# Gated mix on one core: nine stores of x moved behind the first burst of W', the last burst moved to piece 27, the rounding of sums and of u moved

## The chip, the core and the metric

One core of a Trainium2 chip runs the whole program. The metric is the device time of one execution in microseconds (us); the engines are named as in the profile: PE (TensorE, matmul), PEld (its weight loads), DVE (VectorE), ACT (ScalarE), POOL (GpSimd), SP (SyncE, which here only issues transfers). SPq, ACTq and POOLq are the same engines' instructions that issue transfers.

## What is computed

```python
x = A_x                                              # 1 x 2048 x 640
g = sigmoid((x * gate_w).sum(-1, keepdims=True))
# A: the real part of a DFT along the hidden axis and then the sequence
a, b = einsum("bsd,ed->bse", x, dft_hid_re), einsum("bsd,ed->bse", x, dft_hid_im)
y = einsum("ts,bse->bte", dft_seq_re, a) - einsum("ts,bse->bte", dft_seq_im, b)
# B: 32 heads pick 2 of 256 experts by keys in two halves
q = einsum("nd,dhc->nhc", x, w_q);  q1, q2 = q[..., :128], q[..., 128:]
s1, s2 = einsum("nhd,ed->nhe", q1, k1), einsum("nhd,ed->nhe", q2, k2)
...                                                  # top 2 of each, top 2 of their sums, softmax -> gates, experts
act = gelu(einsum("nd,nhkd->nhk", x, u[experts]))
out = einsum("nhk,nhk,nhkd->nd", gates, act, v[experts])
result = g * y + (1 - g) * out
```

## The kernel before: how the work is staged

All large products are in fp32, each operand taken apart into a rounded part (h) and a rest (l); a product is three matmuls (`mm3`, lines 138 to 142: h by h, h by l, l by h). ACT makes h, and DVE or POOL subtracts to make l (`split`, lines 133 to 136; the profile shows all of these under L135 and L136).

**The pieces.** The sequence transform is cut into 128 pieces (w, c, s): w is the real or imaginary matrix, c one of four blocks of 512 columns, s one of 16 tiles of 128 rows of x. Piece n (`seq_piece`, line 225) is 15 matmuls of 128x512 (five banks of 128 hidden features, three matmuls each) with x tile s, `X[s]`, as weights. The first four pieces run their matmuls in another order (L240). A column block is done when its 16 pieces are; the banks are then copied by ACT to the staging tile ST (L248), and only then may the next block's matmuls overwrite them. Block c ends with pieces 15, 31, 47 and so on. A piece's W tile (`wf`, 256 KB) is loaded five pieces ahead by SP (L173) and taken apart three pieces ahead into a ring of four places (`WS`).

**Hooks.** `at(n, f)` registers a step, and all steps of piece n are written into the engines' queues right after piece n's matmuls, in the order of registration. Every engine runs its queue strictly in that order. So this table of numbers, and not a scheduler, sets the order of all work around the change. Transfers issued by SP and ACT take turns on eight semaphores: a transfer is issued only after the one that had its semaphore before has landed.

**Before piece 30** the hooks fit in, beside the pieces:

- x: tiles 4 to 15 are loaded by SP (`load_x`, L284, one piece ahead of the split), taken apart by ACT and DVE three pieces before use (`split_x`), and summed for the gate by DVE (`gate_sum`, L314).
- Stores of x: room runs out later, so x tiles 0 to 8 are stored to a scratch in DRAM (`put_x`, L493, 640 KB each) at pieces 6, 8, 10, ..., 22, tiles 9 and 10 at piece 26; `get_x` (L497) loads them back, tiles 0, 1, 2 at pieces 28, 28, 29.
- W' = w_q by keys: 32 loads of 640 KB (`load_wq`, L396, tile `wq` or `wqu`) feed four bursts of eight (`w_part`, L405, 64 small matmuls) after pieces 10, 16, 22 and 28. Two banks take turns, and DVE transposes each pair of parts out of its bank into `wp` (L411) before the bank is used again. A burst makes two groups G of W'. Some loads borrow the room of an x tile: the last three (29, 30, 31) take those of X6, X7, X8.
- `split_w` takes group G apart into WH, WL (the profile's WU). For groups 4 to 7 `make_t` draws four sums and differences from W' (tile `tt`, one buffer; six DVE operations, L433 to L438) and takes each apart (tiles `tw`, in the room of X0 to X5, and a part of WU).
- u: five tiles are loaded (`load_u`, L446, two buffers) at pieces 22 to 26 and taken apart (`split_u`, tile UU) at pieces 24 to 28.
- x transposed: loaded at piece 22 (`load_xT`, L461), split at 27 (tiles xh, xl), and four sums of it are made by DVE at piece 28 (`sum_xT`, L480 to L483).

After piece 31 the first score products run on PE (`score_step`), between pieces 31 and 32 six matmuls of WU by xh and xl. From there on 16 tiles of scores, top-k picks, experts and the hidden transform run beside the rest of the pieces.

Of the kernel before, what the change touches and what calls it, by code (L numbers as in the profile page):

```python
# [8 lines left out]
F32 = mybir.dt.float32  # L9
# [8 lines left out]
P = 128  # L18
# [14 lines left out]
NG = HH // 8  # L33
# [73 lines left out]
def gated_mix_kernel(ctx: ExitStack, tc: tile.TileContext, xT, xn, dreT, dimT, wsre, wsim, wq, kT, uT, vv, gw, out):  # L107
# [14 lines left out]
    def bank(n, shape=(P, TC), dt=F32):  # L122
        return psum.tile(list(shape), dt, name=f"b{n}", tag=f"b{n}")

    def ps_t(shape, dt=F32):
        return bank(7, shape, dt)
# [6 lines left out]
    def split(f, h, l, eng):  # L133

        nc.scalar.activation(h, f, AF.Copy)  # L135
        eng.tensor_sub(l, f, h.bitcast(F32))  # L136
# [55 lines left out]
    def at(n, f, *args):  # L192
        then.setdefault(n, []).append(lambda: f(*args))
# [57 lines left out]
    for q in range(2 * NC):  # L251
        n = NT * (q + 1)
# [10 lines left out]
    p1 = p1_stack.enter_context(tc.tile_pool(name="p1", bufs=1, reuse_waits="tile"))  # L263
# [72 lines left out]
    t = ps_t([P, TC])  # L336
    for n in range(WARM):
        c = slice(0, 2 * P) if n < WARM - 1 else slice(2 * P, TC)
# [43 lines left out]
    NWQ = 4 * NG  # L382
    BURST = 8
# [14 lines left out]
    def w_part(m):  # L398
        G, n, r = m // 4, m // 2 % 2, m % 2
        if r == 0:  # L400
            wps[G, n] = bank(5 + n)
        ps = wps[G, n]
        w = wqs.pop(m)
        for j in range(4):
            nc.tensor.matmul(ps[32 * j:32 * j + 32, :HALF], kp[:, 8 * G // H, r, :], w[:, j], start=(r == 0),  # L405
                             stop=(r == 1))
        if r == 1:
            if n == 0:
                wp[G] = p1.tile([P, KD, P], F32, name="wp", bufs=2)
            t = wp[G].rearrange("p k (j c) -> p j k c", c=32)[:, 2 * n:2 * n + 2]  # L410
            nc.vector.transpose(t, wps.pop((G, n))[:, :HALF].rearrange("p (j k c) -> p j k c", j=2, c=32))  # L411
# [3 lines left out]
        k = slice(0 if G < NG // 2 else 2, KD)  # L415
        split(wp[G][:, k], WH[:, k, c], WL[:, k, c], nc.vector)

    TW, LEFT = {}, []

    def make_t(G):  # L420


        if not TW:
            f = [big.tile([P, 2 * D], F32R, name="tw", tag=f"X{n}") for n in range(6)]
            TW.update((n, [t[:, :PAIR].rearrange("p (k c) -> p k c", k=2) for t in f[2 * n - 2:2 * n]])
                      for n in (1, 2, 3))
            LEFT.extend(t[:, PAIR:] for t in f)
            TW[4] = WH[:, :2, TC:], WL[:, :2, TC:]
        c = slice(P * (G - NG // 2), P * (G - NG // 2 + 1))
        b12, b22 = (wp[G][:, k:k + 2] for k in (0, 2))  # L430
        (b11h, b21h), (b11l, b21l) = ([w[:, k:k + 2, c].bitcast(F32) for k in (0, 2)] for w in (WH, WL))
        t = p1.tile([P, 4, 2, P], F32, name="tt", tag="tt")
        nc.vector.tensor_sub(t[:, 0], b12, b11h)  # L433
        nc.vector.tensor_sub(t[:, 2], b22, b12)
        nc.vector.tensor_sub(t[:, 0], t[:, 0], b11l)
        nc.vector.tensor_sub(t[:, 1], b22, t[:, 0])
        nc.vector.tensor_sub(t[:, 3], b21h, t[:, 1])
        nc.vector.tensor_add(t[:, 3], t[:, 3], b21l)  # L438
        for n in range(1, 5):
            split(t[:, n - 1], *(w[:, :, c] for w in TW[n]), nc.vector)  # L440

# [54 lines left out]
        X[s] = place(tag)  # L496
        nc.sync.dma_start(X[s].bitcast(F32), xd[s])  # L497

    for s in range(9):
        at(6 + 2 * s, put_x, s)  # L500
    for s, tag in ((11, "xh"), (12, "xl")):
        at(s + 12, move_x, s, tag)
    for n in range(NT - 4):
# [5 lines left out]


    n = N0 - 1
    for B in range(NWQ // BURST):
        b = 10 + 6 * B
        for m in range(BURST * B, BURST * (B + 1)):
            at(b, w_part, m)
        for a in range(2):
            G = 2 * B + a
            at(b + (a if b < n - 1 else 0), split_w, G)
            if G >= NG // 2:
                at(min(b + 1, n - 1) + a, make_t, G)  # L520
    for b, m in enumerate((0, 1, 2, 3, 4, 5, 6, 7, 8)):
        at(b, load_wq, m)
    for m, b in enumerate((10, 10, 11, 11, 12, 12, 13, 14, 16, 16, 16, 17, 18, 19, 20, 20, 22, 22, 22, 22, 23, 24, 25), 9):
        at(b, load_wq, m)
    for s in range(9, AWAY):
        at(n - 3, put_x, s)
    for s, b in enumerate((28, 28, 29)):
        at(b, get_x, s, 6 + s)
    at(n - 7, load_xT, 0)
    for k in range(KD):  # L530
        at(n - 7 + k, load_u, k)
        at(n - 5 + k, split_u, k)
    for a in range(2):
        at(n - 2, split_xT, 0, a)
    at(n - 1, sum_xT, 0)
# [268 lines left out]
    for p in range(NP):  # L804
        n = N0 + 4 * p + min((p + 1) // 2, 3)
# [3 lines left out]
    for n in range(2 * NT + 3, 4 * NT + 3):  # L809
        s = n % NT  # L810
# [269 lines left out]
    for k, (n, m) in enumerate(((-1, 2), (0, 4), (5, 7), (7, 9), (10, 12))):  # L1080
        n, m = NT * (NC + 2) + n, NT * (NC + 2) + m
# [253 lines left out]
```

## Time and profile before

| | us |
|---|---|
| median of 3 runs | 756.03 |
| lowest and highest of them | 753.8 and 756.59 |
| the profiled execution's own time | 754.75 |
| its span (first to last instruction) | 753.0 |
| PE busy | 743.4 |
| DVE busy | 577.6 |
| ACT busy, POOL busy | 366.1, 341.7 |

A row of the timeline has start and duration in us, engine, line, operation, the tiles as out<-in, the shape and a count, and in brackets how long the engine stood idle before it and what ended that. Matmuls overlap, so a matmul's duration is longer than the distance to the next one. A row of the chain of waits has start, duration and what the time went to.

### The profile page before, as it was taken

Reading aid. Unit: us, or ns where it says so; the run is one execution under the profiler, and the core shown is the slowest. Engines: PE = TensorE matmul, PEld = TensorE weight load, DVE = VectorE, ACT = ScalarE, POOL = GpSimd, SP = SyncE. Lnnn points to the kernel's source line nnn. Section 1 sums busy time; section 2 is a strip of 40 time slices with the busy share of each in tenths; the row PEclk is TensorE's granted clock in tenths of the full one; section 3 lists DMA queues with packets and bytes.
Section 4 is the critical chain, followed back from the end, with each engine's and each line's share of the span. In section 5 each row is a group of like instructions: output and inputs, shape, how many; then the busy total and the mean of one; then the engine's idle time right before and its main releaser. Section 6 shows DMA issues by size and latency. Waiting matters only on the chain.

```text
span 753.0 us, 11145 instructions
## 1 busy us (share of the span) xinstructions
PE 743.4 (99%) x3923; PEld 604.8 (80%) x3923; DVE 577.6 (77%) x744; ACT 366.1 (49%) x664; POOL 341.7 (45%) x287
## 2 busy tenths in 40 slices
PE   9989999899999999999999999999999999999998
PEld 7857877688888888888888888888888888888887
DVE  7871364576899899999999888979899984357651
ACT  4334244542444755564553587533555653443451
POOL 5532433441523334244135555644456793487253
PEclk9999999999999999999999999999999999999999
DMA  9999979588575786863398766388856689775301
GB/s 340 407 399 340 380 303 342 163 245 251 146 205 129 177 262 162 220 173 124 102 353 308 188 157 191 111 265 293 297 184 196 222 268 352 210 243 171 111 29 71
DMA packets 84632, 171.11 MB, mean 227 GB/s; under 512 B 16096, under 2 KB 21600, under 8 KB 84320
## 3 DMA queue, kind: packets, MB, share of 16 engines
q1 hardware_dynamic: 70960, 146.13, 56.6%
q0 software_dynamic: 5472, 9.96, 8.4%
q10 hardware_dynamic: 8144, 14.31, 5.2%
q8 instruction: 31, 0.51, 0.3%
q14 instruction: 25, 0.20, 0.1%
HBM read 136.40 MB, written 32.39 MB: 224 GB/s over the span
## 4 chain that ended last, share of the span: by engine, by line
PE 91%; DMA 4%; DVE 3%; issue 1%; ACT 0%; SPq 0%; ACTq 0%
PE b L140 30%; PE b L142 29%; PE b L141 29%; PE b L405 2%; DMA xr<-in_xn 2%; DMA wq<-in_wq 1%; PE b L888 1%; DMA wf<-in_wsre 1%; DVE xr L314 1%; DVE X L136 0%; DVE WU L136 0%; ACT X L135 0%; DVE xf L481 0%; DVE wp L411 0%; DVE tw L136 0%
## 5 line engine op out<-in xcount | busy, mean ns | idle before, releaser
L140 PE MATMUL b<-WS,X 128*128 128x512 f32 x620 | 243.0, 392 | 2.5 <-ACT ST L248 2.5
L141 PE MATMUL b<-WS,X 128*128 128x512 f32 x620 | 241.3, 389 | 0.0
L142 PE MATMUL b<-WS,X 128*128 128x512 f32 x620 | 241.3, 389 | 0.0
L136 POOL TENSOR_TENSOR WS<-wf,WS 128x512 fp32r<-128x512 f32 x89 | 133.2, 1499 | 173.0 <-ACT WS L135 171.8
L140 PEld LDWEIGHTS b<-WS,X 128*128 128x128 f32 x620 | 116.4, 188 | 29.0 <-ACT ST L248 2.9
L142 PEld LDWEIGHTS b<-WS,X 128*128 128x128 f32 x620 | 116.4, 188 | 24.3
L141 PEld LDWEIGHTS b<-WS,X 128*128 128x128 f32 x620 | 116.4, 188 | 23.8
L135 ACT ACTIVATE WS<-wf 128x512 fp32r<-128x512 f32 x89 | 55.7, 626 | 84.1 <-PE b L142 55.6
L876 DVE TENSOR_TENSOR hot<-rows,wtab 128x1024 f16<-128x1024 f16 x64 | 57.9, 931 | 4.4 <-PE b L888 4.4
L136 POOL TENSOR_TENSOR xl<-xf,xh 128x640 fp32r<-128x640 f32 x16 | 26.8, 1675 | 73.5 <-ACT xh L135 67.1
L598 ACT ACTIVATE sc<-b 128x512 f32<-128x512 f32 x32 | 19.9, 621 | 78.8 <-PE b L142 75.0
L187 POOL DMA_DIRECT2D WS<-in_wsre x30 | 26.4, 880 | 60.6 <-ACT WS L185 59.3
L136 POOL TENSOR_TENSOR WS<-ra,WS 128x512 fp32r<-128x512 f32 x33 | 46.7, 1424 | 14.4 <-ACT WS L135 12.4
L846 ACT ACTIVATE b<-b,mask 128x128 f32<-128x128 f32 x128 | 43.1, 343 | 15.0 <-PE b L888 11.8
L135 ACT ACTIVATE WS<-ra 128x512 fp32r<-128x512 f32 x47 | 29.4, 631 | 42.4 <-PE b L142 28.2
L653 DVE TENSOR_TENSOR eq<-sc,mm 128x1024 f16<-128x1024 f32 x32 | 44.4, 1387 | 0.9
L660 DVE TENSOR_REDUCE tied<-eq 128x64 f32<-128x1024 f16 x32 | 39.0, 1218 | 0.9
L651 DVE TENSOR_REDUCE mm<-sc 128x64 f32<-128x1024 f32 x32 | 38.7, 1210 | 0.2
L213 DVE SCALAR_TENSOR_TENSOR ST<-ST,grow 128x512 f32<-128x512 f32 x40 | 30.4, 820 | 6.0 <-DMA grow<-gdr 4.7
L136 POOL TENSOR_TENSOR WP<-ra,WP 128x512 fp32r<-128x512 f32 x13 | 19.0, 1471 | 31.2 <-ACT WP L135 31.2
L876 DVE TENSOR_TENSOR hot<-hot,rows 128x1024 f16<-128x1024 f16 x32 | 31.5, 985 | 0.0
L140 PE MATMUL b<-WU,xh 128*128 128x512 f32 x80 | 31.2, 391 | 0.0
(218 smaller groups left out, 1442.9 us busy)
## 6 DMA issues: line engine op xcount, KB each, us to landing
X<-xd SPq DMA_DIRECT2D x36, 640.0 KB, 6.2
wq<-in_wq SPq DMA_DIRECT2D x28, 640.0 KB, 9.2
wf<-in_wsim SPq DMA_DIRECT2D x64, 256.0 KB, 4.7
wf<-in_wsre SPq DMA_DIRECT2D x63, 256.0 KB, 6.4
ra<-pd SPq DMA_DIRECT2D x40, 256.0 KB, 3.1
pd<-ST ACTq DMA_DIRECT2D x35, 256.0 KB, 3.9
WS<-in_wsre POOLq DMA_DIRECT2D x30, 256.0 KB, 6.0
xd<-X SPq DMA_DIRECT2D x11, 640.0 KB, 8.6
```

Source lines behind the costliest of these rows:

```text
L135: nc.scalar.activation(h, f, AF.Copy)
L136: eng.tensor_sub(l, f, h.bitcast(F32))
L140: nc.tensor.matmul(o, wh, ah, start=first, stop=False, skip_group_check=more)
L141: nc.tensor.matmul(o, wh, al, start=False, stop=False, skip_group_check=more)
L142: nc.tensor.matmul(o, wl, ah, start=False, stop=last, skip_group_check=more)
L187: nc.gpsimd.dma_start(l, (wsre, wsim)[w][c, s], accum_op=OP.add)
L213: nc.vector.scalar_tensor_tensor(f, f, -1.0 if w else 1.0, g, op0=OP.mult, op1=OP.mult)
L651: nc.vector.tensor_reduce(m, sc, op=OP.max, axis=AX.X)
L653: nc.vector.tensor_tensor(eq, sc, m[:, :, None].to_broadcast([P, HH, E]), op=OP.is_equal)
L660: nc.vector.tensor_reduce(tied[:, s, ib, :], eq, op=OP.add, axis=AX.X)
L846: nc.scalar.activation(f[:, :, n], f[:, :, n], AF.Copy, scale=mask4[:, n:n + 1])
L876: nc.vector.tensor_tensor(o, a, b, op=op)
```

## The change

The nine stores of x tiles 0 to 8 move from pieces 6, 8, ..., 22 to pieces 11, 12, 14, 15, 17, 18, 19, 20, 21. The last burst moves from after piece 28 to after piece 27. Both groups of a burst are taken apart at the burst's own piece. `make_t` is cut in two: the sums of group G are drawn at piece b or b + 1 and are taken apart one piece later (`split_t`). The u tiles are loaded at pieces 20 to 24 and taken apart at 22 to 26. Tile 0 of x is loaded back at piece 27 (1 and 2 stay at 28 and 29). No work is added or left out.

```diff
     def make_t(G):
...
-        t = p1.tile([P, 4, 2, P], F32, name="tt", tag="tt")
+        tts[G] = t = p1.tile([P, 4, 2, P], F32, name="tt", tag="tt")
...
+    def split_t(G):
+        c, t = slice(P * (G - NG // 2), P * (G - NG // 2 + 1)), tts.pop(G)
         for n in range(1, 5):
             split(t[:, n - 1], *(w[:, :, c] for w in TW[n]), nc.vector)
...
-    for s in range(9):
-        at(6 + 2 * s, put_x, s)
+    for s, b in enumerate((11, 12, 14, 15, 17, 18, 19, 20, 21)):
+        at(b, put_x, s)
...
-    for B in range(NWQ // BURST):
-        b = 10 + 6 * B
+    for B, b in enumerate((10, 16, 22, 27)):
         for m in range(BURST * B, BURST * (B + 1)):
             at(b, w_part, m)
-        for a in range(2):
-            G = 2 * B + a
-            at(b + (a if b < n - 1 else 0), split_w, G)
+        for G in (2 * B, 2 * B + 1):
+            at(b, split_w, G)
             if G >= NG // 2:
-                at(min(b + 1, n - 1) + a, make_t, G)
+                at(b + G % 2, make_t, G)
+                at(b + G % 2 + 1, split_t, G)
...
-    for s, b in enumerate((28, 28, 29)):
+    for s, b in enumerate((27, 28, 29)):
         at(b, get_x, s, 6 + s)
...
-        at(n - 7 + k, load_u, k)
-        at(n - 5 + k, split_u, k)
+        at(n - 9 + k, load_u, k)
+        at(n - 7 + k, split_u, k)
```

Lines behind `make_t` move by two or three in the numbering (L493 becomes L496, L446 becomes L449, L480 becomes L483). On PE alone one thing moves: the 15 matmuls of piece 28 stand behind the last burst and no longer ahead of it. POOL's queue stays as it is, and behind piece 32 every queue does.

The first place is SP's queue from piece 8 to the first burst at piece 10. Before (xd<-X is a store of an x tile, xr the load of one, here of tiles 12, 13 and 14; wqu and wq are loads for W', wf a W tile):

```order
L493 DMA xd<-X 128x1280
L284 DMA xr<-in_xn 128x640
L396 DMA wqu<-in_wq 128x1280
L173 DMA wf<-in_wsre 128x512
L284 DMA xr<-in_xn 128x640
L173 DMA wf<-in_wsre 128x512
L493 DMA xd<-X 128x1280
L284 DMA xr<-in_xn 128x640
L396 DMA wq<-in_wq 128x1280 x2
```

The same place now:

```order
L284 DMA xr<-in_xn 128x640
L396 DMA wqu<-in_wq 128x1280
L173 DMA wf<-in_wsre 128x512
L284 DMA xr<-in_xn 128x640
L173 DMA wf<-in_wsre 128x512
L284 DMA xr<-in_xn 128x640
L396 DMA wq<-in_wq 128x1280 x2
L173 DMA wf<-in_wsre 128x512
L496 DMA xd<-X 128x1280
```

The stores of pieces 8 and 10 (and the one of piece 6, further up) are gone from in front of the x loads; the first store now stands behind the two wq loads and the W tile that follow.

The second place is DVE's queue after the last burst. Before, from the rounding of group 6's sums (tw and WU<-tt) on; xf are the sums of x transposed:

```order
L136 TENSOR_TENSOR tw<-tt,tw 128x2x128 x3
L136 TENSOR_TENSOR WU<-tt,WU 128x2x128
L136 TENSOR_TENSOR WU<-wp,WU 128x3x128
L136 TENSOR_TENSOR UU<-uf,UU 128x256
L480 TENSOR_TENSOR xf<-xf 128x256
L481 TENSOR_TENSOR xf<-xf 128x256
L482 TENSOR_TENSOR xf<-xf 128x256
L483 TENSOR_TENSOR xf<-xf 128x256
L433 TENSOR_TENSOR tt<-wp,WU 128x256
L434 TENSOR_TENSOR tt<-wp 128x256
L435 TENSOR_TENSOR tt<-tt,WU 128x256
L436 TENSOR_TENSOR tt<-wp,tt 128x256
```

The same place now:

```order
L136 TENSOR_TENSOR WU<-wp,WU 128x3x128
L136 TENSOR_TENSOR tw<-tt,tw 128x2x128 x3
L136 TENSOR_TENSOR WU<-tt,WU 128x2x128
L433 TENSOR_TENSOR tt<-wp,WU 128x256
L434 TENSOR_TENSOR tt<-wp 128x256
L435 TENSOR_TENSOR tt<-tt,WU 128x256
L436 TENSOR_TENSOR tt<-wp,tt 128x256
L437 TENSOR_TENSOR tt<-WU,tt 128x256
L438 TENSOR_TENSOR tt<-tt,WU 128x256
L483 TENSOR_TENSOR xf<-xf 128x256
L484 TENSOR_TENSOR xf<-xf 128x256
L485 TENSOR_TENSOR xf<-xf 128x256
```

Group 7's sums (the second run of L433 to L438) now stand ahead of the sums of x transposed, and the rounding of u is no longer in between.

The third place is SP's queue around the third burst at piece 22, where the loads for the last burst and those of u stand. Before (xf is x transposed, uf a tile of u):

```order
L493 DMA xd<-X 128x1280
L396 DMA wq<-in_wq 128x1280 x4
L461 DMA xf<-in_xT 128x640 x2
L446 DMA uf<-in_uT 128x256
L173 DMA wf<-in_wsre 128x512
L396 DMA wq<-in_wq 128x1280
L446 DMA uf<-in_uT 128x256
```

Now:

```order
L496 DMA xd<-X 128x1280
L449 DMA uf<-in_uT 128x256
L173 DMA wf<-in_wsre 128x512
L396 DMA wq<-in_wq 128x1280 x4
L464 DMA xf<-in_xT 128x640 x2
L449 DMA uf<-in_uT 128x256
L173 DMA wf<-in_wsre 128x512
L396 DMA wq<-in_wq 128x1280
L449 DMA uf<-in_uT 128x256
```

Two u loads moved ahead of the four wq loads, so the u load behind x transposed is now the third, which waits for a buffer of the two.

More of the change, by code (lines that the diff above doesn't have):

```diff
@@ L416, in split_w @@
         split(wp[G][:, k], WH[:, k, c], WL[:, k, c], nc.vector)
-    TW, LEFT = {}, []
+    TW, LEFT, tts = {}, [], {}
     def make_t(G):
```

## The prediction, made before the changed kernel was run

> **What bounds the kernel now.** I read the page's first part, then who PE waited for, then the places of those waits in the timeline, and the chain of waits at each.
>
> ```profile
> span 753.0 us, 11145 instructions
> PE 743.4 (99%) x3923; PEld 604.8 (80%) x3923; DVE 577.6 (77%) x744; ACT 366.1 (49%) x664; POOL 341.7 (45%) x287
> ```
> ```profile
> PE b L405 <- DVE wp L411: 3.0, 1, 3.0
> PE b L140 <- ACT ST L248: 2.5, 1, 2.5
> PE b L339 <- PEq L1327: 0.8, 1, 0.8
> ```
>
> PE is the bound, and in all it stood still three times: 0.8 us at the start, once in a W' burst, and once before a matmul that wanted a bank. The change adds and removes no matmul, so what it can win is at most those two stalls. The timeline places them:
>
> ```profile
> 18.76 0.39 PE L140 MATMUL b<-WS,X 128*128 128x512 f32 x1
> ...
> 42.34 0.39 PE L142 MATMUL b<-WS,X 128*128 128x512 f32 x1
> 42.65 2.36 PE L405 MATMUL b<-wq,kp 128*32 128x320 f32 x32
> 48.05 1.82 PE L405 MATMUL b<-wq,kp 128*32 128x320 f32 x24 [3.03 <-DVE wp L411]
> ```
> ```profile
> 137.00 0.39 PE L142 MATMUL b<-WU,xl 128*128 128x512 f32 x1
> 139.85 0.50 PE L140 MATMUL b<-WS,X 128*128 128x512 f32 x1 [2.46 <-ACT ST L248]
> ```
>
> The first stands in the middle of the first burst (3.03 us), the second ahead of piece 32 (2.46 us). Between 18.76 and 42.34 lie seven pieces, 105 matmuls, so one every 23.58 / 104 = 0.227 us and 3.40 us a piece; I use this pace below. 3.03 + 2.46 = 5.49 us is 0.73% of the time. A measurement of this kernel can tell about 0.5% (3.8 us) from no change, so both stalls must go for a clear gain.
>
> The chain of waits at the first stall:
>
> ```profile
> 36.77 8.43 DMA xr<-in_xn
> ...
> 45.23 0.75 ACT X L135
> ...
> 45.99 0.83 DVE X L136
> 46.82 0.73 DVE xr L314
> ...
> 47.56 0.44 DVE wp L411
> ...
> 48.05 2.36 PE b L405 x32
> ```
>
> PE waits for a transpose that frees the bank. DVE's queue has x tile 13's subtraction and tile 12's gate sum ahead of that transpose, and tile 13 landed at 45.20. Nothing on PE or DVE is slow here: a load of x is late. The transfers in that stretch (20 to 60 us):
>
> ```profile
> DMA packets 5073, 16.19 MB, mean 405 GB/s; under 512 B 565, under 2 KB 565, under 8 KB 5069
> ...
> xd<-X SPq DMA_DIRECT2D x5, 640.0 KB, 9.1
> ```
>
> The chain at the second stall, from the last transpose of the last burst to the bank's copy:
>
> ```profile
> 121.16 4.49 PE b L405 x64
> 125.68 0.52 DVE wp L411
> ...
> 131.75 0.34 DVE UU L136
> 132.09 0.35 DVE xf L480
> ...
> 134.35 0.42 DVE xf L483
> 134.78 0.34 DVE tt L433
> ...
> 136.74 0.44 DVE tt L438
> ...
> 139.22 0.59 ACT ST L248
> ```
>
> DVE works without a gap from 125.68 to 137.18. ACT can round group 7's sums only when DVE has made them, and the copies of the banks (L248) stand behind that rounding in ACT's queue. PE wanted the bank right after 137.00.
>
> **Part 1: the stores behind the first burst.** The stores of pieces 6 and 8 leave the queue ahead of x tile 13 (that of piece 10 stood behind it already). Each is 640 KB, 655,360 bytes; at 405 GB/s that is 1.62 us, two 3.24 us. The queue is full over this stretch and lands in order, so I let tile 13 land 3.24 us earlier, at 41.96. ACT is free by then: its row for piece 13's W tile was held behind x tile 12, which comes earlier by the same two stores.
>
> ```profile
> 42.17 0.74 ACT L135 ACTIVATE X<-xr 128x640 fp32r<-128x640 f32 x1 [3.33 <-DMA xr<-in_xn]
> 42.82 0.61 ACT L135 ACTIVATE WS<-wf 128x512 fp32r<-128x512 f32 x1
> ```
>
> These move to 38.93 and 39.58; the ring place that the second wants is free once piece 9 has run, at 42.65 - 3.40 = 39.25. Then the chain above runs as it stands, 3.24 us earlier: the transpose ends at 48.00 - 3.24 = 44.76. PE asks for the bank at 42.65 + 2.36 = 45.01. So the stall goes, with 0.25 us to spare: **-3.03 us**, and the bound on the other side is what the margin is worth (below, the gate sum).
>
> **Part 2: the end of the stage.** Two things shift against each other. PE: before, pieces 29, 30, 31 and six matmuls lay between the burst and the demand, 51 x 0.227 = 11.6 us; now piece 28 lies there too, 66 x 0.227 = 15.0 us. DVE and ACT: from the last transpose's start to the end of the first bank's copy went 139.81 - 125.68 = 14.1 us. The rounding of u (0.34) and the four sums of x transposed (134.78 - 132.09 = 2.69) no longer stand ahead of group 7's sums; that leaves 14.1 - 3.0 = 11.1. The copy would be ready 3.9 us ahead of the demand: **-2.46 us**. What is late next is the copy's own source, the bank that PE itself finishes in piece 31, and that costs nothing as the copies follow PE bank by bank. The five stores that ACT issues at piece 28 now stand behind the last W' rounding; two of them wait for transfers that SP issues behind the burst. I take nothing for that: it has the 3.9 us as cover, and costs what goes beyond it.
>
> **Part 3: what moves into the middle.** The stores don't vanish. From piece 17 to 21 there are five, one a piece; a piece then carries 640 + 640 + 256 KB for stores, W' and W. That is 1,572,864 bytes, 3.88 us at 405 GB/s against 3.40 us of PE: the queue grows by 0.5 us a piece, 2.4 us in all. The third burst needs load 23, the first of these two:
>
> ```profile
> 81.00 1.97 SPq L396 DMA_DIRECT2D wq<-in_wq  x2
> ```
> ```profile
> DMA to landing us min/median/max: 10.8/11.2/11.6
> ```
> ```profile
> 96.10 4.44 PE b L405 x64
> ```
>
> It landed at 91.8; its matmuls are the last eighth of the burst, at 96.10 + 3.9 = 100.0. Of these 8.2 us the earlier PE takes 3.0 and the fuller queue 2.4; 2.8 are left. Cost 0, on the other side 1 us if my queue is off by half again. W tiles are loaded five pieces (17 us) ahead: 0.
>
> The last burst comes 3.40 us earlier against its loads, and 3.03 for the first stall. Its last load, 31:
>
> ```profile
> 111.95 0.43 SPq L396 DMA_DIRECT2D wq<-in_wq  x1
> ```
> ```profile
> DMA to landing us min/median/max: 5.8/5.8/5.8
> ```
>
> It landed at 117.8 and was wanted at 121.16 + 3.9 = 125.1. Now it is wanted at 125.1 - 3.4 - 3.0 = 118.7, so even if it doesn't move with the rest it is in time by 0.9 us; it should move, since it waits for piece 24 on PE, and u loads that are ahead of it run on DVE's work of the same earlier pieces. Cost 0. The u rounding moves to pieces 22 to 26, among stretches in which DVE waited:
>
> ```profile
> 113.39 0.43 DVE L136 TENSOR_TENSOR UU<-uf,UU 128x256 fp32r<-128x256 f32 x1 [2.32 <-ACT UU L135]
> ```
>
> Five at 0.43 us fit into waits like that one. Rounding both groups at the burst's own piece on DVE only swaps neighbours. Moving the reload of x tile 0 to piece 27 costs nothing: it stays behind the burst that frees its room, and is wanted at piece 32.
>
> **The sum.** 754.75 (the profiled execution's own time, 1.75 over its span) - 3.03 - 2.46 = 749.3 us. The profiled execution was a quick one: the median of the three runs is 1.28 over it, and the mean of all four 755.3. From that mean: 755.3 - 5.5 = **749.8 us**, my number.
>
> **Rivals.**
>
> *The gate sum holds the transpose.* The same operation takes two times on DVE:
>
> ```profile
> 43.69 1.90 DVE L314 CUSTOM_DVE_ANT_0 xr<-xr,gwb 128x640 f32<-128x640 f32 x1
> ...
> 46.74 0.82 DVE L314 CUSTOM_DVE_ANT_0 xr<-xr,gwb 128x640 f32<-128x640 f32 x1
> ```
> ```profile
> 43.51 1.40 POOL L136 TENSOR_TENSOR WS<-wf,WS 128x512 fp32r<-128x512 f32 x1 [2.40 <-ACT WS L135]
> 49.76 1.29 POOL L136 TENSOR_TENSOR WS<-wf,WS 128x512 fp32r<-128x512 f32 x1 [4.85 <-ACT WS L135]
> ```
>
> 1.90 us where a subtraction runs on POOL, 0.82 where POOL is idle, as it was for tile 12's sum. If the earlier x loads push that sum onto POOL's subtraction, the transpose comes 1.08 us later, and with 0.25 us to spare 0.8 us of the first stall stays: 750.6. Against it: ACT's rounding ahead of that subtraction moves up as well, by my times POOL is done at 39.58 + 0.69 + 1.40 = 41.7 and the sum starts at 46.74 - 3.24 = 43.5. [...] Chance 0.10.
>
> *One stall stays whole.* If x tile 13 is held by something else than the queue's length (a buffer, a semaphore), the first stall stays: 755.3 - 2.5 = 752.8. If ACT is held at its five stores for over 3.9 us, the second does: 752.3. For it: margins of 0.25 and 3.9 us are thin against landings of 8 us. Chance 0.11.
>
> *The gain is given back.* The fuller queue lets the third burst wait for load 23 by as much as was won: 755.3. This takes 8 us more lateness than I find. Chance 0.06.
>
> *Slower: the last burst waits for load 31.* SP issues in order, and each of the last three loads stands behind a u load that waits for DVE to have done with an older u tile:
>
> ```profile
> SPq L446 <- DVE UU L136: 3.6, 3, 1.9
> ```
>
> That was 3.6 us in all. DVE now has the sums of groups 4 and 5 around these roundings. If each of the three waits grew to 4 us (a group's sums take 2.4, 134.78 to 137.18, and their rounding comes on top), load 31 would be issued 8.4 us later than now, less the 3.0 of the earlier PE: it lands at 123.2 against 118.7, and 4.5 us of the 5.5 are lost. It turns slower once load 31 lands later than 118.7 + 5.5 = 124.2; with waits of 6 us it lands at 129.2, 10.5 late: 760.3. Against it: in the old order DVE was through with groups 4 and 5 by 113.39 and idle ahead of a u tile (the row above). Chance 0.05.
>
> That the change doesn't do what it says is ruled out by the order: no store stands ahead of tile 13 any longer.
>
> **How the numbers follow.** Both stalls go: 0.68, about 749.8, with 1 us of unknown cost above and the scatter of the runs (753.8 to 756.59) about it. Of that, some 0.08 would show as less than 0.5%. Gate sum: 0.10, nearly all still faster. One stall stays: 0.11, within 0.5%. Given back: 0.06, within. Slower: 0.05. So faster 0.69, same 0.26, slower 0.05. The range goes from 753.8 - 5.5 - 0.5 = 747.8 up to 753.0, over the case of one stall; it leaves out the last two cases.
>
> **What would show it.** Right: PE waits only for its start, the first burst takes 4.4 us as the others do, x tile 13 lands near 42, and the matmul behind the score products has no wait. Wrong: a row of PE waiting for L411 at the first burst (the gate sum at 1.90 beside it or the x load late), for L248 ahead of piece 32, or for `wq` at 93 to 97 or 114 to 119 us. A stall of over 1 us anywhere on PE behind 140 us would mean that work beside the pieces lived on the old delays.

## The result and the profile after

750.11 us median of 6 executions (749.8 to 750.29), before 755.95 us median of 6 (753.8 to 756.98): the ratio is 0.9927, 95% interval 0.9912 to 0.9942. The profiled execution took 750.29 us with a span of 748.5; that of before took 754.75 with 753.0. The two traces thus differ by 4.46 us, the two medians by 5.84. Both numbers need an explanation.

The page of after, its first lines, and who PE waited for (us in total, times, the longest):

```profile
span 748.5 us, 11144 instructions
...
PE 743.3 (99%) x3923; PEld 604.3 (81%) x3923; DVE 579.4 (77%) x744; ACT 365.3 (49%) x664; POOL 342.6 (46%) x287
```
```profile
PE b L140 <- ACT ST L248: 1.1, 2, 0.7
PE b L339 <- PEq L1329: 0.8, 1, 0.8
```

PE's busy time is what it was (743.4 before), so the 4.5 us came out of PE's waits. The wait for L411 is gone. The wait for a bank copy (L248) is still there, twice now, 1.1 us in all.

**The first stall is gone, by the predicted chain.** PE at the first burst, and ACT and DVE ahead of it:

```profile
42.42 3.98 PE L405 MATMUL b<-wq,kp 128*32 128x320 f32 x56
46.22 0.72 PE L405 MATMUL b<-wqu,kp 128*32 128x320 f32 x8
46.87 0.50 PE L140 MATMUL b<-WS,X 128*128 128x512 f32 x1
```
```profile
41.56 0.74 ACT L135 ACTIVATE X<-xr 128x640 fp32r<-128x640 f32 x1 [1.75 <-DMA xr<-in_xn]
```
```profile
42.34 0.83 DVE L136 TENSOR_TENSOR X<-xr,X 128x640 fp32r<-128x640 f32 x1 [0.42 <-ACT X L135]
43.08 0.82 DVE L314 CUSTOM_DVE_ANT_0 xr<-xr,gwb 128x640 f32<-128x640 f32 x1
...
43.82 0.51 DVE L411 STREAM_TRANSPOSE wp<-b 128x320 f32<-128x320 f32 x1
```

ACT starts on x tile 13 at 41.56, where before it started at 45.23: the tile landed 3.67 us earlier (predicted 3.24). The gate sum ahead of the transpose took 0.82 us, not the 1.90 of the rival, and the transpose was there at 43.82 for a bank that PE wanted near 42.42 + 2.36 = 44.78 (2.36 is what a burst's first 32 matmuls took before).

**A wait that was not there before.** PE at piece 16:

```profile
64.81 0.50 PE L140 MATMUL b<-WS,X 128*128 128x512 f32 x1 [0.65 <-ACT ST L248]
```

The chain of waits behind it, and ACT at the same place before:

```profile
44.62 8.97 DMA xd<-X
...
53.68 9.85 DMA wf<-in_wsre
...
63.64 0.63 ACT WS L135
64.27 0.49 ACT ST L248
```
```profile
64.32 0.63 ACT L135 ACTIVATE WS<-wf 128x512 fp32r<-128x512 f32 x1 [1.24 <-PE b L142]
64.95 2.64 ACT L248 ACTIVATE ST<-b 128x512 f32<-128x512 f32 x4
```

The first of the moved stores took 8.97 us to land. The load of a W tile was issued behind its landing, took 9.85 us itself, and its rounding stands ahead of the bank copies in ACT's queue. Before, the same rounding ran at 64.32 and was itself waiting for PE, which was 3 us later then. That W tile (the 18th load of its kind in both traces) was issued at 52.64 before and landed 10.3 us later, at 62.9, which left it 1.4 us; now it landed at 63.5, and PE was some 3 us earlier. So the moved stores made a W tile 0.6 us late where the earlier PE had used up the slack.

**The second stall shrank from 2.46 to 0.48 us.** PE ahead of piece 32, then ACT (ACTq rows are the issuing of DMAs), DVE and POOL behind the last burst:

```profile
134.52 0.39 PE L142 MATMUL b<-WU,xl 128*128 128x512 f32 x1
135.39 0.50 PE L140 MATMUL b<-WS,X 128*128 128x512 f32 x1 [0.48 <-ACT ST L248]
```
```profile
122.21 0.74 ACT L135 ACTIVATE xh<-xf 128x640 fp32r<-128x640 f32 x1 [1.34 <-DMA xd<-X]
122.37 0.83 ACTq L223 DMA_DIRECT2D pd<-ST  x2
...
123.23 0.61 ACTq L223 DMA_DIRECT2D pd<-ST  x1
...
123.88 2.68 ACTq L223 DMA_DIRECT2D pd<-ST  x2
126.61 1.04 ACT L135 ACTIVATE tw<-tt 128x256 fp32r<-128x256 f32 x3 [2.50 <-issue]
```
```profile
123.05 0.55 DVE L136 TENSOR_TENSOR WU<-wp,WU 128x384 fp32r<-128x384 f32 x1
127.06 1.69 DVE L136 TENSOR_TENSOR tw<-tt,tw 128x256 fp32r<-128x256 f32 x3 [3.46 <-ACT tw L135]
128.67 1.50 DVE L136 TENSOR_TENSOR WU<-tt,WU 128x256 fp32r<-128x256 f32 x1
```
```profile
123.03 3.52 POOL L136 TENSOR_TENSOR xl<-xf,xh 128x640 fp32r<-128x640 f32 x2 [5.79 <-ACT xh L135]
126.51 1.29 POOL L136 TENSOR_TENSOR WS<-wf,WS 128x512 fp32r<-128x512 f32 x1
128.55 1.34 POOL L136 TENSOR_TENSOR WS<-wf,WS 128x512 fp32r<-128x512 f32 x1 [0.76 <-ACT WS L135]
```

DVE, which had no gap here before, stands 3.46 us: group 6's rounding on ACT comes late, behind five stores whose issuing takes 4.1 us (0.83 + 0.61 + 2.68) and behind a rounding of x transposed that waited for a landing. When DVE goes on, its operations run beside POOL's subtractions and take 1.69 and 1.50 us. Before, the same rows took 1.09 and 0.42:

```profile
129.86 1.09 DVE L136 TENSOR_TENSOR tw<-tt,tw 128x256 fp32r<-128x256 f32 x3
130.86 0.42 DVE L136 TENSOR_TENSOR WU<-tt,WU 128x256 fp32r<-128x256 f32 x1
```

From the start of the last transpose (119.79) to the end of the first copy (135.34) that makes 15.55 us instead of the predicted 11.1. The demand came 15.0 us after the burst, as predicted, so half a microsecond of the stall was left.

In the traces: -3.03 - 2.46 + 0.65 + 0.48 = -4.36 us, of 4.46 measured.

**A margin thinner than I thought.** The last burst and its last loads in the trace of after:

```profile
L405 PE MATMUL b<-wq,kp x64: 432/432/457, 115.2 to 119.3; 128*32 128x320 f32 x64
L396 SPq DMA_DIRECT2D wq<-in_wq x2: 382/402/423, 109.6 to 111.3; - x2
...
DMA to landing us min/median/max: 4.5/5.8/7.1
```

Load 31 was issued at 111.3 and landed at 118.4; the last eighth of the matmuls began at 115.2 + 56/63 x 4.1 = 118.8. PE did not wait, but with 0.4 us to spare, not 0.9. The load did not move with PE as I had thought it should: it was issued 0.7 us earlier than before and took 7.1 us to land instead of 5.8. The rival "slower" was nearer than I had priced it.

### The profile page after: what moved, and what is told of

Its sections match the earlier page's. It is cut to its first block, busy times and chain, and to the rows that moved or that the text cites. A ratio compares the mean times of both kernels' runs of the same rounds, so it can differ in the third digit from the quotient of the medians.

```text
span 748.5 us, 11144 instructions
## 1 busy us (share of the span) xinstructions
PE 743.3 (99%) x3923; PEld 604.3 (81%) x3923; DVE 579.4 (77%) x744; ACT 365.3 (49%) x664; POOL 342.6 (46%) x287
## 4 chain that ended last, share of the span: by engine, by line
PE 92%; DMA 5%; DVE 2%; SPq 0%; ACT 0%; issue 0%; ACTq 0%; DVEq 0%
PE b L140 29%; PE b L142 29%; PE b L141 29%; DMA xd<-X 2%; PE b L240 2%; DMA wf<-in_wsre 2%; PE b L405 1%; PE b L890 1%; DMA pd<-ST 1%; DVE WU L136 0%; PE b L339 0%; DVE tt L436 0%; DVE tw L136 0%; SPq L173 0%; DVE UU L136 0%
## 5 line engine op out<-in xcount | busy, mean ns | idle before, releaser
L142 PE MATMUL b<-WU,xl 128*128 128x512 f32 x80 | 31.1, 389 | 0.0
```

The source lines that it names most:

```text
L142: nc.tensor.matmul(o, wl, ah, start=False, stop=last, skip_group_check=more)
```

## The experiments

The theory after the result: the stores alone remove the first stall, the earlier burst with the new rounding order alone removes the second, and what is left over comes from the moved stores (piece 16) and from ACT's own five stores (piece 32). The rivals: the gain lies elsewhere than in these stalls, or the second stall is set by the late transfers and by POOL, not by who issues ACT's stores. The last question, opened by the first experiments, was why medians move by more than the stalls do.

**e0: the kernel before, a second profile.** No edit.

> The kernel before, profiled a second time, to see where its scatter of 3.2 us (753.8 to 756.98) lies. Theory: in the two stalls, so that first plus second stall differ from 5.5 us by as much as this execution's time differs from 754.75. Rival: the stalls are 3.0 and 2.5 again and the difference lies elsewhere.

756.03 us. PE's stalls are 2.3 and 2.7 us, 0.5 us less than in the first trace, and yet this execution took 1.28 us longer. Behind the first stall its second row of the burst (24 matmuls) took 3.43 us, against 1.82 us for the same 24 in the first trace of before. The windows show why (the columns are the window, its length, the busy time of PE, PEld, DVE, ACT and POOL with their instructions, the granted clock, the DMA share and GB/s):

```profile
47.42 3.43 PE L405 MATMUL b<-wq,kp 128*32 128x320 f32 x24 [2.27 <-DVE wp L411]
```
```profile
44.00:48.00 4.00, 1.73 (x28) 0.53 (x23) 3.35 (x7) 0.94 (x2) 0.27 (x1) 0.92 1.03 396
48.00:52.00 4.00, 4.00 (x35) 1.70 (x28) 1.02 (x3) 1.78 (x3) 1.27 (x1) 0.65 1.02 403
```

The granted clock falls behind the stall. Work lost, in full-clock time: 0.08 x 4.00 + 0.35 x 4.00 = 1.72 us. In the first trace both windows stand at 1.00. So the time of before is not its stalls alone: some executions pay a clock drop on top. The theory as stated failed here, and the drop was added to it.

**e1: the stores alone.** Against before:

```diff
-    for s in range(9):
-        at(6 + 2 * s, put_x, s)
+    for s, b in enumerate((11, 12, 14, 15, 17, 18, 19, 20, 21)):
+        at(b, put_x, s)
```

> Only the nine stores moved, the rest as before. Theory: the first stall goes (3.0 to 0), the new wait before piece 16 is there (about 0.6), the second stall stays (2.5): 3.0 - 0.6 = 2.4 us faster in the profiled execution, about 752.4. Rival (the first stall went because both groups of a burst are now rounded at once): the first stall stays at 3.0 and there is no gain.

753.55 us (12 executions, 753.14 to 754.25), ratio 0.9963 (0.9949 to 0.9978). In its profile the first stall is gone, PE waits 0.45 us ahead of piece 16 and 2.62 ahead of piece 32. So the new wait at piece 16 belongs to the stores, and the second stall to the other part. Behind the second stall the clock drops here:

```profile
136.00:140.00 4.00, 3.01 (x8) 2.41 (x9) 3.04 (x5) 4.00 (x11) 2.52 (x3) 0.66 0.39 56
```

**e2: all but the stores.** Against after:

```diff
-    for s, b in enumerate((11, 12, 14, 15, 17, 18, 19, 20, 21)):
-        at(b, put_x, s)
+    for s in range(9):
+        at(6 + 2 * s, put_x, s)
```

> Everything changed but the stores, which stay at pieces 6, 8, ..., 22. Theory: the first stall stays at 3.0, there is no wait before piece 16, and the second stall is 0.5 or less: 2.0 to 2.5 us faster in the profiled execution, about 752.5. Rival: the second stall went only because PE came to it earlier or the transfers were differently placed, so it stays over 1.5 us here and the gain is under 1 us.

754.11 us (12 executions, 752.34 to 756.1), ratio 0.9972 (0.9954 to 0.999). First stall 3.6 us, with a clock drop behind it; second 0.6; none ahead of piece 16. Alone, the two parts bring 2.26 and 1.70 us in the medians, together 5.84: more than their sum, since each alone leaves a stall of 2.6 us or more, behind which the clock can still drop. Both profiled executions took longer than expected (753.2 us for 752.4, 755.3 for 752.5): their stalls came within 0.6 us of what was expected, but the theory had no clock drops.

**e3: one store of the two.** Against before:

```diff
-        at(6 + 2 * s, put_x, s)
+        at(11 if s == 1 else 6 + 2 * s, put_x, s)
```

> As before, but the store of piece 8 alone goes behind the burst (piece 11). Theory (each store ahead of x tile 13 costs 1.6 us of a full queue): x tile 13 lands 1.6 us earlier and the first stall is 3.0 - 1.6 = 1.4 us; second stall 2.5 as before; 753.1. Rival (the tile waits for a buffer or a semaphore): the first stall stays at 3.0, or goes whole with the one store.

754.07 us (753.01 to 754.61), ratio 0.9973 (0.9958 to 0.9987). First stall 0.8 us, second 2.7. With two stores moved the first stall is 0, with one 0.8, with none 2.3 to 3.6 over the traces. The stall goes with the bytes ahead of x tile 13, as the theory wants; one store is worth rather more than the 1.62 us that its bytes give at 405 GB/s (3.0 - 0.8 = 2.2 from the first trace, 1.5 from the second).

**e4: the earlier burst alone.** The order of the sums, the roundings and u stays as before:

```diff
-        b = 10 + 6 * B
+        b = 10 + 6 * B - B // 3
...
-    for s, b in enumerate((28, 28, 29)):
+    for s, b in enumerate((27, 28, 29)):
```

> As before, but with the last burst at piece 27 (and the reload of x tile 0 with it); the order of roundings, u and the stores stay. Theory (ACT is held some 3.5 us by its five stores ahead of group 6's rounding, which the old order of DVE can't afford): 14.1 + 3.5 us of chain against 15.1 us until the demand, so 2 to 3 us of the second stall stay; first stall 3.0; no gain, about 754.5. Rival (the earlier burst alone is enough): second stall 0.5 or less, about 752.5.

755.95 us (753.82 to 757.88), ratio 0.9991 (0.9976 to 1.0006): no gain. The second stall stays at 2.3 us although PE has a piece more to do. DVE and POOL there:

```profile
124.77 1.79 DVE L433 TENSOR_TENSOR tt<-wp,WU 128x256 f32<-128x256 f32 x1
126.49 1.78 DVE L434 TENSOR_TENSOR tt<-wp 128x256 f32<-128x256 f32 x1
128.20 1.51 DVE L435 TENSOR_TENSOR tt<-tt,WU 128x256 f32<-128x256 f32 x1
```
```profile
124.49 3.50 POOL L136 TENSOR_TENSOR xl<-xf,xh 128x640 fp32r<-128x640 f32 x2 [4.49 <-ACT xh L135]
127.96 1.47 POOL L136 TENSOR_TENSOR WS<-wf,WS 128x512 fp32r<-128x512 f32 x1
```

Three sums of 0.42 us take 1.79, 1.78 and 1.51, since they fall on POOL's subtractions. A piece earlier, the burst's sums meet the rounding of x transposed, which did not move with it. The expectation had the outcome right and the cause wrong: it put the wait down to ACT's five stores, but ACT was through with issuing them at 126.84 and came to group 6's rounding only when DVE had made three of the sums:

```profile
129.74 1.19 ACT L135 ACTIVATE tw<-tt 128x256 fp32r<-128x256 f32 x3 [4.18 <-DVE tt L435]
```

In these rows the first two sums last about as long as POOL's two subtractions (3.50 us for both), the third about as long as the next one (1.47). With the changed order (e2, same late burst) the six sums take 0.41 to 0.43 us each and are done at 127.96, before POOL starts at 128.38, and the stall was 0.6. Why they last that long beside POOL was not shown.

**e5: ACT's five stores issued by SP.** Against after:

```diff
-        eng = nc.sync if q == 2 * NC - 1 else nc.scalar
+        eng = nc.sync if q in (0, 2 * NC - 1) else nc.scalar
```

> The changed kernel, with the five stores of the first column block issued by SP instead of ACT. Theory: ACT comes to group 6's rounding some 3.5 us earlier, the 0.48 us left of the second stall goes, and the 0.65 us before piece 16 stays: 0.5 us faster than the changed kernel, 749.6. Rival (DVE, slowed by POOL's subtractions, holds the chain): the 0.48 us stays within 0.2, 750.1.

750.62 us (749.95 to 750.92), ratio 0.9929 (0.9913 to 0.9944): as after. The wait ahead of piece 32 goes from 0.48 to 0.27 only. ACT is 1.6 us earlier, and DVE loses it again:

```profile
125.00 1.01 ACT L135 ACTIVATE tw<-tt 128x256 fp32r<-128x256 f32 x3
```
```profile
125.44 3.59 DVE L136 TENSOR_TENSOR tw<-tt,tw 128x256 fp32r<-128x256 f32 x3 [1.37 <-ACT tw L135]
128.95 1.51 DVE L136 TENSOR_TENSOR WU<-tt,WU 128x256 fp32r<-128x256 f32 x1
```

DVE starts 1.6 us earlier and is done no earlier (130.46 against 130.17), because it runs beside POOL longer (3.59 us instead of 1.69). ACT's issuing was one thing that held DVE, POOL the next. The expected 749.6 was missed: the theory was right about ACT, and the rival about the time.

**e6: the second store at piece 14, not 12.** Against after:

```diff
-    for s, b in enumerate((11, 12, 14, 15, 17, 18, 19, 20, 21)):
+    for s, b in enumerate((11, 14, 15, 16, 17, 18, 19, 20, 21)):
```

> The changed kernel, with the second store at piece 14 instead of 12 and the third to fifth at 15, 16, 17 and 18 in turn, so that W tile 18 has one store of 1.6 us fewer ahead of it. Theory: W tile 18 lands about 1.6 us earlier, the 0.65 us before piece 16 goes, the 0.48 us stays: 749.5. Rival (the gate's table load or its sum holds ACT there): the 0.65 us stays, 750.1.

749.38 us (5 executions, 748.86 to 749.5), ratio 0.9912 (0.9895 to 0.9929). The W tile comes 1.65 us earlier and PE doesn't wait at piece 16; ahead of piece 32 it waits 0.19 us:

```profile
61.99 0.63 ACT L135 ACTIVATE WS<-wf 128x512 fp32r<-128x512 f32 x1 [1.68 <-DMA wf<-in_wsre]
```
```profile
PE b L339 <- PEq L1329: 0.8, 1, 0.8
PE b L140 <- ACT ST L248: 0.2, 1, 0.2
```

This beats both kernels: 0.73 us under after in the medians, with no overlap of the executions, though the intervals of the two ratios overlap.

**e7: e5 and e6 together.**

> Both of the last two edits. Theory: no wait on PE but its start, 750.1 - 0.65 - 0.48 = 749.0. Rival: one of the two waits comes back in another place, 749.5 or more.

749.57 us (748.73 to 750.25), ratio 0.9915 (0.9897 to 0.9932): no better than e6, and over the 749.0 of the theory; the rival, a wait in another place, holds. Waits of 0.5 us at the start and 0.3 ahead of piece 32.

**e8 to e11: a stall of chosen length.** From e6, work that nothing needs is put on DVE inside the second burst: 3, 4, 5 or 6 subtractions on a tile (gwb) that is read no longer there. PE then waits for DVE as it did in the first stall. The theory comes from the traces so far: behind a stall of 2.3 us (e0, e4) or more the clock can drop, which took about 1.7 us of full-clock work each time in e0, e1, e2 and e4 (1.60 to 1.72 by the windows), and it need not (the first trace of before has stalls of 3.0 and 2.5 us and no drop). For three subtractions it gives no drop, 749.4 + 1 = 750.4 us and a scatter under 1 us.

```diff
+            if m == 9:
+                for _ in range(3):
+                    nc.vector.tensor_sub(gwb, gwb, gwb)
```

> The kernel of the second store later (no stall over 0.2 us), with three DVE operations of 0.82 us added between the first and the second transpose of the second burst, so that PE stands still about 1 us there. [...]

> The same with four operations, a stall of about 1.8 us. Theory: at the edge; 751.2, with a second group of times 1.7 us above in at most a third of the executions. Rival: 751.2, scatter under 1 us.

> The same with five operations, a stall of about 2.6 us. Theory: two groups of times, 751.9 and 753.6, each with a good part of the executions. Rival: one group at 751.9, scatter under 1 us.

> The same with six operations, a stall of about 3.4 us. Theory: the drop in nearly every execution, 754.4 with few at 752.7. Rival: one group at 752.7, scatter under 1 us.

| subtractions | longest stall in the profile | clock drop in it | profiled, us | all executions, us | ratio |
|---|---|---|---|---|---|
| 3 | 1.3 | none | 751.66 | 751.23 to 752.83, median 751.6 | 0.9949 (0.9934 to 0.9964) |
| 4 | 2.2 | none | 752.14 | 751.31 to 754.94, median 753.54 | 0.9966 (0.9952 to 0.9979) |
| 5 | 3.1 | one | 755.13 | 752.43 to 755.85, median 754.86 | 0.9983 (0.9968 to 0.9998) |
| 6 | 3.9 | one of double length | 756.19 | 755.03 to 757.5, median 756.17 | 1.0007 (0.9996 to 1.0018) |

PE behind the stall with four and with five subtractions, and the granted clock with five and with six:

```profile
72.95 0.75 PE L405 MATMUL b<-wqu,kp 128*32 128x320 f32 x8 [2.20 <-DVE wp L411]
73.51 0.72 PE L405 MATMUL b<-wq,kp 128*32 128x320 f32 x8
```
```profile
74.11 1.27 PE L405 MATMUL b<-wqu,kp 128*32 128x320 f32 x8 [3.06 <-DVE wp L411]
75.14 1.31 PE L405 MATMUL b<-wq,kp 128*32 128x320 f32 x8
```
```profile
74.00:78.00 4.00, 3.89 (x21) 1.95 (x22) 1.85 (x5) 1.68 (x3) 0.00 (x0) 0.57 0.99 312
```
```profile
74.00:78.00 4.00, 3.14 (x18) 1.34 (x19) 1.92 (x5) 0.90 (x2) 0.00 (x0) 0.51 0.96 315
78.00:82.00 4.00, 4.00 (x13) 3.11 (x13) 1.34 (x2) 1.10 (x2) 1.39 (x1) 0.64 1.03 416
```

From four to five subtractions the stall grows by 0.9 us and the profiled time by 2.99. PE's waits in all grow by 1.2, and the drop is the rest: 0.43 x 4.00 = 1.72 us of work lost. With four, PE's rows run at the full clock in the profile, but the executions scatter over 3.6 us, where those of e6 lie within 0.64. The mean granted clock of each execution tells them apart: five at 1.000 average 752.53 us, seven at 0.997 or 0.998 average 754.04.

The stalls came 0.3 to 0.5 us longer than expected, and drops were more common. With four operations 7 of 12 executions are below 0.999, where at most a third were expected to be slow; with five 10 of 12, with six all 12, and with three none of six. Those six scatter over 1.6 us all the same, so drops are not the only scatter.

**One account for all profiles.** Time = e6's 749.38, plus PE's waits in the waits view beyond the start's 0.8 us and e6's 0.2, plus 1.7 us for each clock drop that the windows show:

| kernel | waits, us | drops | account | measured |
|---|---|---|---|---|
| before, first trace | 5.5 | 0 | 754.7 | 754.75 |
| before, second (e0) | 5.0 | 1 | 755.9 | 756.03 |
| after | 1.1 | 0 | 750.3 | 750.29 |
| e1 stores alone | 3.1 | 1 | 754.0 | 753.2 |
| e2 all but the stores | 4.2 | 1 | 755.1 | 755.3 |
| e3 one store | 3.5 | 0 | 752.7 | 753.03 |
| e4 burst alone | 5.6 | 2 | 758.2 | 757.1 |
| e5 stores by SP | 0.8 | 0 | 750.0 | 750.57 |
| e7 both | 0.8 | 0 | 750.0 | 749.8 |
| e8 | 2.7 | 0 | 751.9 | 751.66 |
| e9 | 3.0 | 0 | 752.2 | 752.14 |
| e10 | 4.2 | 1 | 755.1 | 755.13 |
| e11 | 4.2 | 2 | 756.8 | 756.19 |

Nine of thirteen come within 0.33 us; e5 comes out 0.6 us too low and e11 0.6 too high. The mean granted clock of the core says the same: 1.000 in each trace without a drop, 0.998 with one, 0.995 with two. The two that are furthest off, e1 and e4, both too high, are those with a drop behind the second stall; there ACT is busy for the whole window (4.00 of 4.00 in the row of e1), so PE may have had to wait in that stretch anyway. That is argued, not shown. The executions point the same way: in e3, where the second stall is the only one over 0.8 us, those with a drop take 0.84 us more in the mean (seven against five), while in e2, where the first is the only one, those at 0.997 or 0.998 take 2.3 us more (five against five).

**The clock of every execution of before.** The mean granted clock is on record for each execution, traced or not. Over the 74 executions of before that ran beside e0 to e11:

| mean granted clock | executions | mean time, us |
|---|---|---|
| 1.000 | 25 | 754.55 |
| 0.997 or 0.998 | 32 | 756.16 |
| 0.995 | 12 | 757.61 |
| 0.993 | 5 | 759.37 |

By the steps of the traces (0.998 with one drop, 0.995 with two), two thirds of the executions of before have at least one drop, and each step goes with about 1.6 us. All six of after stand at 1.000, with a mean of 750.10 us. Without drops the two kernels are thus 4.45 us apart, which is what the stalls of the traces come to.

## Why the prediction was right, and which steps were not

The number, 749.8 us, stands 0.3 us from the measured 750.11, and its range held it. The mechanism was right: both stalls were what could be won, and the moved stores and the new order of the burst's work took them. That the number came so close is in part luck, as several steps were off and made up for one another.

- **First stall, -3.03: right in mechanism and size.** Tile 13 came 3.67 us earlier rather than 3.24; the gate sum took 0.82 us, so that rival did not occur. e1 and e3 show that the stores do it.
- **"W tiles are loaded five pieces (17 us) ahead: 0": failed.** 0.65 us at piece 16. The 17 us are not slack: the load waited for a store to land (8.97 us) and then took 9.85 us, 18.8 in all. Even before, the tile was ready only 1.4 us ahead of its rounding. e2 has no such wait, e1 has it, and e6 removes it with one number in the table.
- **Second stall, -2.46: too much by 0.48.** The step that failed is "I take nothing for that: it has the 3.9 us as cover" for ACT's five stores. The cover was used up by things of which I had named the first only: ACT's issuing and, ahead of it, a landing that the rounding of x transposed waits for (together DVE stands 3.46 us), and DVE's operations falling beside POOL's subtractions (3.19 us for 1.51). e5 takes the issuing away: DVE then stands 1.37 us, and the time beside POOL grows instead. The prediction had named the sign, a row of PE waiting for L248 ahead of piece 32, and it came.
- **Part 3, the fuller queue at the third burst and load 31: right at 0**, the second with 0.4 us to spare.
- **The base: mis-sized.** I put the profiled execution's being 1.28 us below the median down to scatter, and took the mean of four, 755.3. The median over more executions was 755.95. The trace of before was one without a clock drop, while the second trace of the same kernel has one, worth 1.72 us. So against the profiled execution the change is worth 4.46 us, and in the medians another 1.4, since it also takes away the stalls behind which the clock drops. My sum had 5.49 from the stalls where 4.36 came; the missing 1.1 was made up by drops that I did not have. This is the luck in the number.

The part of the drops in the medians rests on the granted clock of each execution, in the table above: executions of before without a drop are 4.45 us over after, as the stalls say, and the others lie about 1.6 us higher for each drop. Kernels whose stalls are all under 0.8 us (after, e5, e6, e7) have no execution below 0.999 and scatter by 0.5 to 1.5 us, while the 29 executions of before beside e0 go from 753.98 to 759.59. How long the stalls were in an execution without a trace is not known.

## What to carry to other kernels

Price a stall of the bounding engine by its length and by what the clock does behind it (here about 1.7 us of full-clock work for each drop); one trace may show neither a drop nor its cost, so a profiled execution that is quicker than its median is a thing to explain. Slack counted in pieces is no slack until the load's own issue is followed back: here a load "17 us ahead" stood behind a store for 9 us, and had had 1.4 us to spare. And moving a step on one engine a piece earlier moves it against all that did not move with it: look what runs beside it there, here POOL's subtractions above all (a sum of 0.42 us took 1.79 beside one in e4).

## What the runs showed of the hardware

**A clock drop behind a short stall of PE.** A drop takes about 1.7 us of full-clock work (1.60 to 1.72) out of one window of 4 us or two neighbouring ones (3.40 in e11). PE runs at about half its rate in it: the rows of 8 matmuls above take 1.31 us (e10) against 0.72 (e9), the first window of e11's drop stands at 0.51, and behind the second stall of e4 the matmuls of 128x512 follow one another at 0.43 us instead of 0.227, from 141.59 to 144.15:

```profile
141.59 0.63 PE L141 MATMUL b<-WS,X 128*128 128x512 f32 x1
142.01 0.63 PE L142 MATMUL b<-WS,X 128*128 128x512 f32 x1
...
143.72 0.62 PE L140 MATMUL b<-WS,X 128*128 128x512 f32 x1
144.15 0.42 PE L141 MATMUL b<-WS,X 128*128 128x512 f32 x1
144.41 0.40 PE L142 MATMUL b<-WS,X 128*128 128x512 f32 x1
```

Over fourteen traces: no stall of 1.3 us or less was followed by one; of those between 2.2 and 3.0 us three were (2.3 in e0, 2.6 in e1, 2.3 in e4) and five were not (3.0 and 2.5 in before, 2.7 in e0, 2.7 in e3, 2.2 in e9); of those of 3.1 us and more all four were (3.1, 3.3, 3.6, 3.9). Length alone does not decide between 2.2 and 3.0 us; what else does was not shown.

**The same DVE operation beside POOL and alone.** 0.42 us alone, 1.50 to 1.79 beside a POOL subtraction (e4, after, e5), so a sum in DVE's queue has two prices, and which holds depends on a schedule that neither engine's own queue shows. Not every operation beside POOL is longer: in before the rounding of u (131.67) and the first sum of x transposed (132.00) take 0.42 us each beside a POOL subtraction of 1.86 us (from 131.71; one with no DVE work beside it, at 117.04, took 1.29), and the next sum takes 1.40.

**Issuing a store.** ACT's five stores cost it 0.83 + 0.61 + 2.68 = 4.1 us in after, the last two of them 2.68. Before, the five took 0.83 + 0.49 + 1.03 = 2.35 us, the last two 1.03:

```profile
123.54 1.03 ACTq L223 DMA_DIRECT2D pd<-ST  x2
```

Other transfers were in flight in both. Why the issue itself grew was not tried.
